# Four units of a linear-attention kernel: keys turned by TensorE instead of loaded as blocks

## The chip, the core and the metric

The kernel runs on one core of a Trainium2 chip. The metric is the device time of one execution in microseconds (us). The time before is 661.25 us, the median of three runs (660.89 to 662.71). The profile is of one further execution.

Names in the rows: PE is TensorE's matmul and PEld its weight load, DVE is VectorE, ACT is ScalarE, POOL is GpSimd, SP is SyncE, which only issues transfers (DMAs).

## The reference

Attention with a complex decay that differs per step and per key dimension, then a two-layer network on its output. B, H, S, D = 4, 8, 768, 48; the network has 3072 rows, width 384 and 2048 hidden units.

```python
mag = sqrt(a_re**2 + a_im**2); scale = minimum(mag, 0.999) / (mag + 1e-6)
ar, ai = a_re * scale, a_im * scale
for t in range(S):                      # per batch and head; S_re, S_im are D x D
    S_re, S_im = (ar[t] * S_re - ai[t] * S_im + outer(k[t], v[t]),
                  ar[t] * S_im + ai[t] * S_re)      # row d of the state turns by a[t, d]
    y[t] = q[t] @ S_re
x = y as rows (b, t) of width H * D
out = gelu(x @ w_in) @ w_out            # gelu with erf
```

All is float32, the weights come as float64.

## The kernel before, in words

**Scan.** Time is cut into eight chunks (two of 64 steps in group 0, two of 64 in group 1, two of 128 in each of the groups 2 and 3). Within a chunk the product of the decays is taken step by step by VectorE (`scan`, tiles `tt` and `bt`), for all 32 lanes of batch and head at once, in 24 slices of 8 steps. Each slice multiplies queries and keys by the product or its inverse (`towards`, `against`, tile `xt`), which makes the decay vanish from the attention inside a chunk, and writes them to a table in device memory (`kq0` to `kq3`, one per group, a row of 2 x 96 numbers per lane and step).

**Units.** The attention proper is done in 24 units: unit u is batch u % 4 and the 128 steps from (u // 4) * 128. So units 8 to 11 are the first four of group 2, units 12 to 15 read the other half of the same table. Function `unit` loads values (`vn`), keys in rows (`kn`, the first half of `kqn`), and needs keys and queries also turned, with the 96 dimensions on partitions: `kT` in the two `kp` tiles and `qT` in the two `qT` tiles, four heads each. Then come the scores (`att<-qT,kp`, eight matmuls, 16 in the records), a multiplication by the causal mask on VectorE (`kp<-att,causal`, one per four heads), the output (`att<-kp,vn`, and `att<-qT,st` for the state), and the keys times values that are added to the batch's state (`att<-vn,kqn`). From unit 6 on the state is first turned by the chunk's gain; for that its halves are exchanged by two DMAs (`m<-st`). The output goes to `xT` as a high and a low part, by ScalarE and VectorE.

**Two ways to turn.** Units under `UDT` = 8 load keys and queries in rows (one DMA, `kqn<-kq`) and turn them by TensorE (`att<-ident_r,kqn`), four heads into a bank of PSUM, with a copy to the `kp` or `qT` tile by ScalarE or VectorE (nested function `turn`). Units from 8 on load both as blocks of 32 x 32 into `blk`, which lies in the memory of `raw_all` (three DMAs of 1024 packets of 128 bytes for keys and three for queries, `raw_all<-kq`), and turn each block on VectorE (`STREAM_TRANSPOSE`). Keys in rows (`kqn<-kq`, 384 KB) are loaded beside that up to unit 19, for the state. `blk` is there once: a unit's blocks can be loaded when the unit before has turned its own.

**Network.** Nine blocks j of 2, 3, 3, 3, 3, 3, 3, 2, 2 units: `ph<-xT,wi` (nine matmuls for each of 16 hidden pieces f), gelu twice on ScalarE (`gh`, `gf`), their difference on VectorE (`gl`), then `po<-wo,gh/gl`. The first matmul of a block needs the `xT` of all of its units: block 3 holds units 8 to 10, block 4 units 11 to 13. In blocks 0 and 1 the units' work and the 32 pieces of the weights are split in high and low parts beside the network's matmuls.

**Order.** Nothing is issued where the code calls it. Class `Plan` records all calls as steps with a cost (`Plan.cost`, for a DMA also `step.data` from its packets and bytes, in `Plan.add`) and with what they wait for. `natural` ranks the steps by the longest way to the end plus an offset per kind of work (table `MORE`), `forward` lets each engine take the best ranked step that is ready, with a choice of engine for copies (`BIAS` weighs the engines), and four passes back and forth keep the order that is best by the planner's own estimate. So every instruction's place on each engine follows from these tables; each engine, SP's queue too, then works strictly in that order. Almost all rows of the profile have the line 422 of `issue`.

The choice between the two ways stands here (lines 825 and 894):

```python
if u < UDT:
    P.sync.dma_start(out=kqn, in_=...)                       # rows
...
if u >= UDT:
    P.vector.transpose(out=t[0:D2], in_=blk[0:D2, c, hh * 4:hh * 4 + 4])
```

Of the kernel before, what the change touches and what calls it, by code (L numbers as in the profile page):

```python
# [20 lines left out]
B, H, S, D = 4, 8, 768, 48  # L21
D2 = 2 * D
BH = B * H
C = 128
# [4 lines left out]
GROUPS = ((0, 64), (128, 64), (256, 128), (512, 128))  # L29
NG = len(GROUPS)  # L30
NP = 2 * NG

UNITS = [[(b, t, C)] for t in range(0, S, C) for b in range(B)]
# [24 lines left out]
def dap(t, offset, dims):  # L58
    return bass.AP(t.tensor, t.offset + offset, dims)
# [9 lines left out]
FIXED = {"vector": 0.075, "scalar": 0.098, "gpsimd": 0.149, "tensor": 0.002, "sync": 0.62}  # L69
# [6 lines left out]
TABLE = 1.3  # L76
ISSUE = 0.9
FETCH = 2.2
PACKET, BYTES = 0.5e-3, 2.96e-6

ROUND, PASS = 0.462e-3, 0.4219e-3

# [10 lines left out]
PASSES = 4  # L93
N_A = 4
WL = 0.307
UDT = 8
FILL, FROM, TO, ONE = 0.6, 50.0, 82.0, 0.217

MORE = dict(lanes0=575.74, lanes1=-377.35, lanes2=-812.79, lanes3=221.09, weights0=-149.78, weights1=-103.19, units0=636.83, units1=1302.69, units2=549.34, blocks0=-201.58, blocks1=340.05, blocks2=534.64, checks=865.08)
BIAS = dict(vector=0.07, scalar=-0.61, gpsimd=7.10)  # L100


def run(x):
# [18 lines left out]
class Plan:  # L122
# [90 lines left out]
    def cost(self, call, outs, ins):  # L213
        engine, name, _, kw = call
        if engine == "sync":
            return FIXED[engine] * (1 if 32 < outs[0].shape[0] < 128 else 0.73)
        size = lambda x: int(math.prod(c for _, c in x.ap[1:]))
        n = max(size(x) for x in outs[:1] + ins)
        each = EACH[engine]
        if engine == "tensor":  # L220
            rows, cols = (kw["lhsT"] if name == "matmul" else kw["in_"]).shape[0], size(kw["lhsT"] if name == "matmul" else kw["in_"])
            if ins[0].dtype == F32R:
                return max(0.06, n * ROUND) + 0.005 * (name == "transpose")
            if name == "transpose":
                return 0.108

            if cols <= 32:
                return max(0.035, n * PASS)
            if cols <= 64:
                return max(0.056, 2 * n * PASS)  # L230
            return max(0.17 if rows > 64 else 0.195, 4 * n * PASS + 0.006)
        elif engine == "vector" and name in ("tensor_scalar", "tensor_copy") and all(x.tensor.space != PSUM for x in ins):
            each /= 2
        t = FIXED[engine] + n * each + (ACCUM[engine] if "accum_out" in kw else 0.0)
        if engine == "scalar":
            if any(x.tensor.space == PSUM for x in ins):
                t -= FROM_PSUM
            if any(size(x) == 1 for x in ins):
                t += POINTER
        elif engine == "gpsimd" and name == "scalar_tensor_tensor":  # L240
            t = FIXED[engine] + n * 1.25e-3
        return t
# [31 lines left out]
    def natural(self):  # L274

        steps = self.steps
        rest = [0.0] * len(steps)
        nextof = {}
        for i in range(len(steps) - 1, -1, -1):
            s = steps[i]  # L280
            e, (_, cost) = next(iter(s.options.items()))
            t = max((rest[j] for j in s.after), default=0.0) + cost + AFTER[e]
            if e == "sync":
                t += ISSUE + FETCH + s.data
            if s.chain is not None:
                if s.chain in nextof:
                    t = max(t, rest[nextof[s.chain]] + cost * s.weight)
                nextof[s.chain] = i
            rest[i] = t
        return [t + MORE[s.kind] for t, s in zip(rest, steps)]  # L290

    def forward(self, rank):
# [14 lines left out]
        while len(order) < len(steps):  # L307
            best = None
            for e, waiting in pool.items():
# [8 lines left out]
                if len(steps[i].options) > 1:  # L318
                    ends = {o: max(free[o], ready[i], port[other[o]] if o in steps[i].port else 0.0) + c + BIAS[o] for o, (_, c) in steps[i].options.items()}
                    if ends[e] > min(ends.values()) + 1e-9:  # L320
# [29 lines left out]
            if e == "sync":  # L350
                channel = end = max(end + FETCH, channel) + s.data
            taken[i] = e, start, cost, end - start
            order.append(i)
            for o in s.options:
# [9 lines left out]
    def backward(self, end, taken, _):  # L364

        steps = self.steps
        left = [len(s.after) for s in steps]
        ready = [end] * len(steps)
        pool = {e: [i for i, s in enumerate(steps) if not s.after and taken[i][0] == e] for e in FIXED}
        free = dict.fromkeys(FIXED, end)  # L370
        starts = [0.0] * len(steps)
        last = lambda some: max(some, key=lambda i: (taken[i][1] + taken[i][3], i))
        for _ in steps:
            best = None
            for e, waiting in pool.items():
                if not waiting:
                    continue
                t = min(free[e], max(ready[i] for i in waiting)) - NEAR
                i = last(i for i in waiting if ready[i] >= t)
                stop = min(free[e], ready[i])  # L380
                if best is None or stop > best[0]:
                    best = stop, i, e
            stop, i, e = best
            pool[e].remove(i)
            starts[i] = free[e] = stop - taken[i][2]
            for j in steps[i].before:
                o, _, cost, whole = taken[j]
                ready[j] = min(ready[j], starts[i] - (ISSUE if "sync" in steps[i].options else AFTER[o]) - (whole - cost))
                left[j] -= 1
                if not left[j]:  # L390
                    pool[o].append(j)
        return starts
# [40 lines left out]
def lanes_and_chunks(ctx, tc, flags, a_lanes, x_lanes, v_units, w_in, w_out, out):  # L433
# [5 lines left out]
    P = Plan(nc, loose=[flags])  # L439
# [44 lines left out]
    kq = [dram.tile([64, c, 2, D2], F32, name=f"kq{g}") for g, (_, c) in enumerate(GROUPS)]  # L484


    apart = [GROUPS[g][1] == C and any(u >= UDT and GROUPS[g][0] <= t < GROUPS[g][0] + 2 * C for u, some in enumerate(UNITS) for _, t, _ in some) for g in range(NG)]

    wide = w_in.dtype == U32
    own = [ps.tile([128, 512], F32, name=f"att{i}", tag=f"att{i}")[:] for i in range(3)]  # L490
# [305 lines left out]
    def unit(u):  # L796
# [3 lines left out]
        chunks, row = [], 0  # L800
        for b, t, n in UNITS[u]:
            for i in range(NP):
                g, m = divmod(i, 2)
# [15 lines left out]
        kqn = next(kqns)  # L819
        kn, qn = kqn[:, :, 0], kqn[:, :, 1]  # L820
        vn = next(vns)
        w = 2 * D2
        _, g, m, _, size, b = chunks[0]
        base, lane = ((m * BH + b * H) * size * w, size * w) if apart[g] else (b * H * 2 * size * w, 2 * size * w)
        if u < UDT:
            P.sync.dma_start(out=kqn, in_=dap(kq[g], base, [[w, C], [lane, H], [1, w]]))
        else:
            for c in range(2):
                for j in range(D2 // 32):
                    P.sync.dma_start(out=blk[j * 32:(j + 1) * 32, c].rearrange("p h (i d) -> p (h i) d", d=32),  # L830
                                     in_=dap(kq[g], base + c * D2 + j * 32, [[w, 32], [32 * w, H * C // 32], [1, 32]]))
            if chunks[-1][0] < NP - 1:
                P.sync.dma_start(out=kn, in_=dap(kq[g], base, [[w, C], [lane, H], [1, D2]]))
        P.sync.dma_start(out=vn, in_=v_units[u])

        held = []
# [54 lines left out]
        qT, kT = [], []  # L891

        def turn(src, dst, ring, halves=(0, 1)):
            if u >= UDT:
                c = 0 if src is kn else 1
                for hh in halves:
                    t = next(ring)
                    P.vector.transpose(out=t[0:D2], in_=blk[0:D2, c, hh * 4:hh * 4 + 4])
                    dst.append(t)
                return  # L900
            some = [next(ps_att) for _ in halves]
            with P.together():
                for hh, p in zip(halves, some):
                    for j in range(4):
                        P.tensor.transpose(out=p[0:D2, j * 128:(j + 1) * 128].bitcast(F32R), in_=src[:, hh * 4 + j, :].bitcast(F32R), identity=ident_r[:])
            for p in some:
                t = next(ring)
                p = p[0:D2, :].rearrange("p (j l) -> p j l", j=4)
                P.either(("scalar", "copy", (t[0:D2], p), {}), ("vector", "tensor_copy", (t[0:D2], p), {}))
                dst.append(t)  # L910
# [73 lines left out]
        j = next(j for j in range(len(BLOCKS)) if u < first_unit[j + 1])  # L984
# [16 lines left out]
    blk = raw_all.rearrange("p i n -> p (i n)").bitcast(F32)[:, 0:16 * C].rearrange("p (c h l) -> p c h l", c=2, h=H)  # L1001
# [63 lines left out]
    for u in range(BLOCKS[0]):  # L1065
        with P.work("units0", f"u{u}"):
            unit(u)
# [250 lines left out]
```

## Time and profile before

| | |
|---|---|
| three runs, us | 661.25 (660.89 to 662.71) |
| profiled execution, us | 664.25 |
| its span, us | 662.2 |
| PE busy | 612.3 us, 92% |
| DVE busy | 482.5 us, 73% |
| ACT busy | 425.7 us, 64% |
| DMA queue 1 | 230720 packets, 100.69 MB, 65.5% of 16 engines' span |
| chain that ended last | PE 59%, DVE 18%, DMA 10%, ACT 8% |

The profiled execution lasts 2.05 us longer than its span. Shares over the whole span mix three stages: in the first VectorE's scan, the weights and the first units run, in the second the rest of the scan with the units from 8 on, in the third the network with the later units. A busy PE is one with a matmul in its records, and its ends are modelled; what an engine waits for is told apart from that in the list of waits.

### The profile page before, as it was taken

What the parts mean: (1) busy time and instruction counts of PE and PEld (TensorE: products, weight loads), DVE (VectorE), ACT (ScalarE), POOL (GpSimd) and SP (SyncE); (2) the same over time, 40 slices, a digit from 0 to 9 for tenths busy, and PEclk for the clock granted to TensorE, in tenths of its full rate; (3) what the DMA queues carried; (4) which work ended last, traced back from release to release, by engine and by line L of the source; (5) the groups of instructions that cost most, each with busy time, mean ns of one, the idle gap of its engine ahead of it and who ended that gap; (6) DMA issues with size and microseconds to landing.
All of it is one profiled execution on the core that took longest, in us unless ns stands there. A gap on an engine that the chain in (4) does not pass through costs nothing.

```text
span 662.2 us, 16181 instructions
## 1 busy us (share of the span) xinstructions
PE 612.3 (92%) x6384; PEld 560.2 (85%) x6384; DVE 482.5 (73%) x1179; ACT 425.7 (64%) x989; POOL 19.9 (3%) x65
## 2 busy tenths in 40 slices
PE   5368799999999999999799999999999999999996
PEld 2136578898899999998788999998899999999995
DVE  7999999998999999998798999436454332342211
ACT  7556678788888888855487887535554544454632
POOL 2001000003000000100100000000000000000000
PEclk9878899999999999999999999999999999999998
DMA  9178967784565556798999796899774570642000
GB/s 295 53 211 216 308 198 199 208 243 131 158 166 127 137 143 163 152 175 152 205 188 211 155 167 172 170 183 148 164 120 113 117 178 4 133 155 73 24 1 28
DMA packets 230801, 101.77 MB, mean 154 GB/s; under 512 B 182080, under 2 KB 223040, under 8 KB 230720
## 3 DMA queue, kind: packets, MB, share of 16 engines
q1 hardware_dynamic: 230720, 100.69, 65.5%
q8 instruction: 51, 0.84, 0.5%
q14 instruction: 30, 0.25, 0.1%
HBM read 74.12 MB, written 23.59 MB: 148 GB/s over the span
## 4 chain that ended last, share of the span: by engine, by line
PE 59%; DVE 18%; DMA 10%; ACT 8%; issue 3%; SPq 2%; DVEq 0%; ACTq 0%
PE po L422 24%; PE ph L422 22%; PE att L422 12%; DVE a L422 4%; DMA m<-st 3%; DVE tt L422 3%; DVE bt L422 2%; DVE xt L422 2%; SPq L422 2%; ACT a L422 2%; DVE tab L422 1%; DMA a<-in_a_lanes_dram 1%; DVE gl L422 1%; DMA kq<-xt 1%; DMA a<-in_moe_w_out_dram 1%
## 5 line engine op out<-in xcount | busy, mean ns | idle before, releaser
L422 PE MATMUL ph<-xT,wi_hi 128*128 128x384 f32 (+1 forms) x864 | 207.7, 321 | 1.9 <-ACT gh L422 1.0
L422 DVE TENSOR_TENSOR gl<-gf,gh 128x384 fp32r<-128x384 f32 (+1 forms) x144 | 73.8, 512 | 121.9 <-ACT gf L422 113.3
L422 PEld LDWEIGHTS ph<-xT,wi_hi 128*128 128x128 f32 x864 | 153.7, 188 | 5.8 <-ACT gh L422 2.0
L422 PE MATMUL ph<-xT,wi_lo 128*128 128x384 f32 (+1 forms) x432 | 137.1, 317 | 0.0
L422 PE MATMUL po<-wo_hi,gh 128*128 128x384 f32 x384 | 132.6, 345 | 3.1 <-ACT ot L422 1.9
L422 ACT ACTIVATE gh<-ph 128x384 fp32r<-128x384 f32 (+1 forms) x144 | 65.3, 455 | 107.8 <-PE ph L422 107.2
L422 PE MATMUL po<-wo_lo,gh 128*128 128x384 f32 x384 | 128.8, 335 | 0.0
L422 PE MATMUL po<-wo_hi,gl 128*128 128x384 f32 x384 | 91.1, 338 | 0.0
L422 PEld LDWEIGHTS ph<-xT,wi_lo 128*128 128x128 f32 x432 | 81.2, 188 | 0.0
L422 PEld LDWEIGHTS po<-wo_hi,gh 128*128 128x128 f32 x384 | 72.2, 188 | 7.3 <-ACT gh L422 3.2
L422 PEld LDWEIGHTS po<-wo_lo,gh 128*128 128x128 f32 x384 | 72.3, 188 | 0.1
L422 ACT ACTIVATE gf<-ph 128x384 f32<-128x384 f32 (+1 forms) x144 | 65.1, 452 | 10.6 <-DVE gl L422 9.1
L422 DVE TENSOR_TENSOR tt<-bt,a 128x192 f32<-128x192 f32 x192 | 68.1, 355 | 0.1
L422 PEld LDWEIGHTS po<-wo_hi,gl 128*128 128x128 f32 x384 | 66.0, 188 | 0.8 <-issue 0.2
L422 ACT ACTIVATE a<-a 128x384 f32<-128x384 f32 (+1 forms) x77 | 41.4, 539 | 20.1 <-DVE a L422 7.9
L422 DVE TENSOR_TENSOR bt<-tt 128x96 f32<-128x96 f32 x192 | 48.8, 254 | 0.1
L422 PEld LDWEIGHTS att<-qT,kp 96*64 96x64 f32 (+1 forms) x512 | 38.8, 164 | 7.4 <-DVE kp L422 4.3
L422 PE MATMUL att<-qT,kp 96*64 96x64 f32 (+1 forms) x512 | 41.4, 251 | 3.9 <-DVE kp L422 3.3
L422 PE MATMUL po<-raw_all,ident_r 128*128 128x384 f32 x64 | 30.4, 557 | 10.2 <-DVE raw_all L422 6.8
L422 DVE TENSOR_TENSOR kp<-att,causal 128x512 f32<-128x512 f32 x48 | 31.9, 686 | 8.2 <-PE att L422 8.0
L422 ACT ACTIVATE a<-a,by_partition 128x384 f32<-128x384 f32 x53 | 33.7, 635 | 1.2
L422 ACT ACTIVATE a<-tab 128x384 f32<-128x384 f32 (+1 forms) x45 | 23.9, 534 | 8.3 <-DVE tab L422 8.2
(157 smaller groups left out, 918.2 us busy)
## 6 DMA issues: line engine op xcount, KB each, us to landing
raw_all<-kq SPq DMA_DIRECT2D x96, 128.0 KB, 4.4
xt<-in_x_lanes_dram SPq DMA_DIRECT2D x24, 384.0 KB, 4.2
kq<-xt SPq DMA_DIRECT2D x48, 192.0 KB, 3.4
a<-in_a_lanes_dram SPq DMA_DIRECT2D x20, 384.0 KB, 4.0
raw_all<-in_moe_w_in_dram SPq DMA_DIRECT2D x16, 384.0 KB, 3.7
raw_all<-in_moe_w_out_dram SPq DMA_DIRECT2D x16, 384.0 KB, 3.8
vn<-in_v_units_dram SPq DMA_DIRECT2D x24, 256.0 KB, 3.7
kqn<-kq SPq DMA_DIRECT2D x8, 768.0 KB, 6.7
```

What stands on the lines that cost most here:

```text
L422: getattr(getattr(self.nc, engine), name)(*args, **kw)
```

## The change

Units 8 to 11 (`QDT` = 8, `KDT` = 12) load only their queries as blocks. Their keys are read in rows, which were loaded before too, and turned by TensorE as in units 0 to 7. From unit 12 on both are blocks as before. The planner's tables change with it: the cost of a packet, the cost of a DMA on SP's queue by kind, the offsets `MORE` and the weights `BIAS`.

```diff
-PACKET, BYTES = 0.5e-3, 2.96e-6
+PACKET, BYTES = 0.6e-3, 2.96e-6
-UDT = 8
+QDT, KDT = 8, 12
-MORE = dict(lanes0=575.74, ...)
+MORE = dict(lanes0=435.30, ...)
-BIAS = dict(vector=0.07, scalar=-0.61, gpsimd=7.10)
+BIAS = dict(vector=0.19, scalar=-0.10, gpsimd=5.92)
@@ def cost
-            return FIXED[engine] * (1 if 32 < outs[0].shape[0] < 128 else 0.73)
+            return FIXED[engine] * (1.06 if outs[0].shape[0] < 128 and outs[0].tensor.name[:3] != 'raw' else 0.73)
@@ def unit
-        if u < UDT:
+        if u < min(QDT, KDT):
             P.sync.dma_start(out=kqn, in_=dap(kq[g], base, [[w, C], [lane, H], [1, w]]))
         else:
-            for c in range(2):
-                for j in range(D2 // 32):
-                    P.sync.dma_start(out=blk[j * 32:(j + 1) * 32, c].rearrange("p h (i d) -> p (h i) d", d=32),
-                                     in_=dap(kq[g], base + c * D2 + j * 32, [[w, 32], [32 * w, H * C // 32], [1, 32]]))
-            if chunks[-1][0] < NP - 1:
-                P.sync.dma_start(out=kn, in_=dap(kq[g], base, [[w, C], [lane, H], [1, D2]]))
+            for c, first in ((0, KDT), (1, QDT)):
+                if u >= first:
+                    for j in range(D2 // 32):
+                        P.sync.dma_start(out=blk[j * 32:(j + 1) * 32, c].rearrange("p h (i d) -> p (h i) d", d=32),
+                                         in_=dap(kq[g], base + c * D2 + j * 32, [[w, 32], [32 * w, H * C // 32], [1, 32]]))
+                if u < first or c == 0 and chunks[-1][0] < NP - 1:
+                    P.sync.dma_start(out=kqn[:, :, c], in_=dap(kq[g], base + c * D2, [[w, C], [lane, H], [1, D2]]))
@@ def turn
-            if u >= UDT:
-                c = 0 if src is kn else 1
+            c = 0 if src is kn else 1
+            if u >= (KDT, QDT)[c]:
```

In the whole program 96 block transfers become 84, 64 VectorE transposes become 56, 128 turns on TensorE become 160, and with them eight more copies out of PSUM; 35 filler matmuls (line 415, issued in planned gaps of PE) become 29. Three places show how the order moves.

SP's queue where units 8 to 10 are fetched, before (`raw_all<-kq2` are blocks, `kqn` keys in rows, `m20<-st` the exchange of a state's halves, `kq3<-xt` a slice's rows of group 3; first row: unit 8's blocks):

```order
L422 DMA raw_all_120<-kq2_107 32x32x32 x6
L422 DMA kqn0_139<-kq2_107 128x8x96
L422 DMA m20_143<-st1_151 48x8x48 x2
L422 DMA kqn1_140<-kq2_107 128x8x96
L422 DMA xt1_133<-in_x_lanes_dram 128x8x96
L422 DMA raw_all_120<-kq2_107 32x32x32 x6
L422 DMA a30_122<-in_a_lanes_dram 128x2x384
L422 DMA m20_143<-st2_152 48x8x48 x2
L422 DMA kqn0_139<-kq2_107 128x8x96
L422 DMA vn0_141<-in_v_units_dram 128x512
L422 DMA raw_all_120<-kq2_107 32x32x32 x6
```

The same place now; unit 8's keys in rows stand just ahead of the first row, and the row of six holds three blocks of unit 12's keys and three of unit 9's queries:

```order
L422 DMA raw_all_120<-kq2_107 32x32x32 x3
L422 DMA kqn1_140<-kq2_107 128x8x96
L422 DMA m20_143<-st0_150 48x8x48 x2
L422 DMA xt1_133<-in_x_lanes_dram 128x8x96
L422 DMA raw_all_120<-kq2_107 32x32x32 x6
L422 DMA a30_122<-in_a_lanes_dram 128x2x384
L422 DMA m20_143<-st1_151 48x8x48 x2
L422 DMA kqn0_139<-kq2_107 128x8x96
L422 DMA vn0_141<-in_v_units_dram 128x512
L422 DMA kq3_108<-xt0_132 32x8x192
L422 DMA kq3_108<-xt0_132 32x8x96 x3
L422 DMA raw_all_120<-kq2_107 32x32x32 x3
```

Each unit's own blocks are half as many, keys in rows stand ahead of them, and a slice's writes have moved in front of unit 10's.

PE ahead of unit 9's scores (the last two rows), before:

```order
L422 MATMUL po0_114<-wo_hi_103,gl1_161 128x384
L422 MATMUL po1_115<-wo_hi_103,gl1_161 128x384
L422 MATMUL po2_116<-wo_hi_103,gl1_161 128x384
L422 MATMUL ph1_113<-xT0_148,wi_hi_101 128x384 x2
L422 MATMUL ph1_113<-xT0_148,wi_lo_102 128x384
L422 MATMUL po0_114<-wo_hi_103,gh0_158 128x384
L422 MATMUL po0_114<-wo_lo_104,gh0_158 128x384
L422 MATMUL ph1_113<-xT0_148,wi_hi_101 128x384 x2
L422 MATMUL ph1_113<-xT0_148,wi_lo_102 128x384
L422 MATMUL att1_110<-qT0_144,kp0_146 128x128 x4
L422 MATMUL att2_111<-qT1_145,kp1_147 128x128 x4
```

And now, from the turns of unit 9's keys (first two rows) on; its scores stand two rows below the last one shown:

```order
L422 MATMUL att0_109<-ident_r_81,kqn1_140 96x128 x4
L422 MATMUL att1_110<-ident_r_81,kqn1_140 96x128 x4
L422 MATMUL po1_115<-wo_hi_103,gh1_159 128x384
L422 MATMUL po1_115<-wo_lo_104,gh1_159 128x384
L422 MATMUL ph1_113<-xT0_148,wi_hi_101 128x384 x2
L422 MATMUL ph1_113<-xT0_148,wi_lo_102 128x384
L422 MATMUL po2_116<-wo_hi_103,gh1_159 128x384
L422 MATMUL po2_116<-wo_lo_104,gh1_159 128x384
L422 MATMUL ph1_113<-xT0_148,wi_hi_101 128x384 x2
L422 MATMUL ph1_113<-xT0_148,wi_lo_102 128x384
L422 MATMUL po0_114<-wo_hi_103,gl1_161 128x384
L422 MATMUL po1_115<-wo_hi_103,gl1_161 128x384
```

The turns are new, with 13 matmuls of the network between them and the scores.

VectorE where unit 8's keys and queries are turned, before:

```order
L422 STREAM_TRANSPOSE qT0_144<-raw_all_120 96x512
L422 STREAM_TRANSPOSE qT1_145<-raw_all_120 96x512
L422 TENSOR_TENSOR bt1_127<-tt1_131 128x2x48
L422 SCALAR_TENSOR_TENSOR tab0_128<-a32_124,tab0_128 128x384
L422 STREAM_TRANSPOSE kp0_146<-raw_all_120 96x512
L422 STREAM_TRANSPOSE kp1_147<-raw_all_120 96x512
L422 TENSOR_TENSOR tt0_130<-bt1_127,a31_123 128x192
L422 TENSOR_TENSOR a30_122<-a30_122 128x384
L422 TENSOR_TENSOR bt1_127<-tt0_130 128x2x48
```

And now:

```order
L422 COPY kp0_146<-att0_109 96x512
L422 COPY kp1_147<-att1_110 96x512
L422 TENSOR_TENSOR bt1_127<-tt1_131 128x2x48
L422 TENSOR_TENSOR a30_122<-a30_122 128x384
L422 STREAM_TRANSPOSE qT0_144<-raw_all_120 96x512
L422 STREAM_TRANSPOSE qT1_145<-raw_all_120 96x512
L422 TENSOR_TENSOR tt0_130<-bt1_127,a31_123 128x192
L422 SCALAR_TENSOR_TENSOR a30_122<-a30_122 128x384
L422 TENSOR_TENSOR gl0_160<-gf0_162,gh0_158 128x384
```

Two transposes out of `raw_all` have become two copies out of PSUM, ahead of the queries' transposes; unit 8's second product with the mask is VectorE's row 738 of the order, where it was row 732.

## Rows read from the trace of the kernel before

**Rows 1.** Busy time in three stretches: us, engines' busy (instructions), PEclk, DMA share, GB/s.

```profile
core 0: us, PE busy (x) PEld busy (x) DVE busy (x) ACT busy (x) POOL busy (x), PEclk, DMA share, GB/s
8.00:284.00 276.00, 249.86 (x2791) 209.94 (x2790) 268.80 (x711) 215.17 (x437) 11.39 (x28) 0.96 0.68 181
284.00:365.00 81.00, 73.90 (x921) 68.34 (x920) 72.96 (x171) 50.24 (x121) 1.73 (x5) 1.00 0.99 187
365.00:655.00 290.00, 286.78 (x2672) 280.89 (x2671) 136.84 (x290) 154.40 (x421) 2.80 (x10) 1.00 0.57 118
```

**Rows 2.** Waits of PE from 280 to 365: us in total, times, longest.

```profile
PE att L422 <- DVE kp L422: 4.2, 6, 2.8
PE ph L422 <- DVE xT L422: 0.6, 1, 0.6
PE att L422 <- DVE qT L422: 0.6, 1, 0.6
PE ph L422 <- ACT gh L422: 0.6, 2, 0.3
PE po L422 <- ACT ot L422: 0.5, 1, 0.5
PE ph L422 <- ACT xT L422: 0.3, 1, 0.3
PE po L422 <- ACT gh L422: 0.2, 1, 0.2
```

**Rows 3.** Timeline of PE: start us, us, what; the wait before unit 11's scores.

```profile
321.61 0.33 PE L422 MATMUL ph<-xT,wi_lo 128*128 128x384 f32 x1
321.79 0.51 PE L422 MATMUL ph<-xT,wi_hi 128*128 128x384 f32 x2
322.13 0.34 PE L422 MATMUL ph<-xT,wi_lo 128*128 128x384 f32 x1
325.28 1.94 PE L422 MATMUL att<-qT,kp 96*128 96x128 f32 x15 [2.81 <-DVE kp L422]
```

**Rows 4.** Timeline of DVE there.

```profile
318.13 0.54 DVE L422 TENSOR_TENSOR xT<-att,xT 128x384 fp32r<-128x384 f32 x1
321.56 1.30 DVE L422 STREAM_TRANSPOSE qT<-raw_all 96x512 f32<-96x512 f32 x2 [2.88 <-DMA raw_all<-kq]
...
324.52 1.29 DVE L422 STREAM_TRANSPOSE kp<-raw_all 96x512 f32<-96x512 f32 x2
```

**Rows 5.** Timeline of SP's queue, the issues for units 8 to 11.

```profile
276.87 4.74 SPq L422 DMA_DIRECT2D raw_all<-kq  x6
281.65 0.86 SPq L422 DMA_DIRECT2D kqn<-kq  x1
...
286.27 7.08 SPq L422 DMA_DIRECT2D raw_all<-kq  x6
...
298.32 7.31 SPq L422 DMA_DIRECT2D raw_all<-kq  x6
...
314.23 6.81 SPq L422 DMA_DIRECT2D raw_all<-kq  x6
```

**Rows 6.** DMA from 280 to 320: queue, packets, MB, share; issues, KB each, us to landing.

```profile
q1 hardware_dynamic: 30090, 6.67, 100.4%
raw_all<-kq SPq DMA_DIRECT2D x19, 128.0 KB, 4.6
kqn<-kq SPq DMA_DIRECT2D x4, 384.0 KB, 5.6
```

**Rows 7.** Groups of one shape: count, busy us, mean ns of one, idle before.

```profile
L422 PE MATMUL att<-ident_r,kqn 128*96 128x128 f32 x128 | 12.0, 234 | 0.4 <-DMA kqn<-kq 0.2
L422 DVE STREAM_TRANSPOSE kp<-raw_all 96x512 f32<-96x512 f32 x32 | 21.5, 694 | 5.3 <-PE att L422 3.5 <-DMA raw_all<-kq 1.5
L422 ACT COPY kp<-att 96x512 f32<-96x512 f32 x16 | 9.0, 584 | 0.9 <-PE att L422 0.4 <-PE po L422 0.3
L422 DVE TENSOR_TENSOR kp<-att,causal 128x512 f32<-128x512 f32 x48 | 31.9, 686 | 8.2 <-PE att L422 8.0 <-ACT wo_hi L422 0.2
```

**Rows 8.** Waits of PE from 365 to 640.

```profile
PE att L422 <- DVE st L422: 1.8, 1, 1.8
PE po L422 <- ACT ot L422: 1.3, 1, 1.3
```

More of the change, by code (lines that the diff above doesn't have):

```diff
@@ L95 @@
 WL = 0.307
-UDT = 8
+QDT, KDT = 8, 12
 FILL, FROM, TO, ONE = 0.6, 50.0, 82.0, 0.217
-MORE = dict(lanes0=575.74, lanes1=-377.35, lanes2=-812.79, lanes3=221.09, weights0=-149.78, weights1=-103.19, units0=636.83, units1=1302.69, units2=549.34, blocks0=-201.58, blocks1=340.05, blocks2=534.64, checks=865.08)
-BIAS = dict(vector=0.07, scalar=-0.61, gpsimd=7.10)
+MORE = dict(lanes0=435.30, lanes1=-370.28, lanes2=-936.27, lanes3=-479.30, weights0=117.89, weights1=28.10, units0=759.67, units1=993.55, units2=658.08, blocks0=-5.01, blocks1=543.97, blocks2=644.37, checks=1304.51)
+BIAS = dict(vector=0.19, scalar=-0.10, gpsimd=5.92)
 def run(x):
@@ L484, in lanes_and_chunks @@
     kq = [dram.tile([64, c, 2, D2], F32, name=f"kq{g}") for g, (_, c) in enumerate(GROUPS)]
-    apart = [GROUPS[g][1] == C and any(u >= UDT and GROUPS[g][0] <= t < GROUPS[g][0] + 2 * C for u, some in enumerate(UNITS) for _, t, _ in some) for g in range(NG)]
+    apart = [GROUPS[g][1] == C and any(u >= min(QDT, KDT) and GROUPS[g][0] <= t < GROUPS[g][0] + 2 * C for u, some in enumerate(UNITS) for _, t, _ in some) for g in range(NG)]
     wide = w_in.dtype == U32
```

## The prediction

> **What bounds the kernel now.** I read the busy time by stretches first, because the shares over the whole span mix three stages [rows 1]. From 8 to 284 us VectorE works 268.8 of 276.0 us: the scan sets the pace, 7.2 us of it are idle. From 284 to 365 us no engine is full (TensorE 73.9 of 81.0, VectorE 73.0), but the DMA share is 0.99. From 365 us on TensorE works 286.8 of 290.0 us and the DMA share is 0.57. The granted clock is 0.96, 1.00 and 1.00, so the upper of the two levels is there nearly throughout.
>
> So the change, which lies around unit 8 to 11, falls into the middle stage, and the list of TensorE's waits says what is lost there: 7.0 us in 13 waits [rows 2]. The largest group is scores that wait for VectorE (`kp`, 4.2 us in six). The longest of them, 2.81 us before unit 11's scores [rows 3], I followed to VectorE: the two transposes of the queries had themselves waited 2.88 us for `raw_all<-kq`, the blocks, and the keys' transposes came after them [rows 4]. The blocks come late for two reasons that the rows show. SP's queue is held 4.74 to 7.31 us by each six block issues [rows 5]. And the queue of transfers is full at 100.4% in 280 to 320 us, with 19 block transfers that land 4.6 us after their issue and four of keys in rows that take 5.6 us [rows 6]. The stage's bound is thus the fetching of blocks, and it costs TensorE, which has more work ready for later, some 7 us.
>
> **Removed.** Twelve block transfers go (three for each of four units); the keys in rows that replace them were loaded before. One block transfer is worth between 4.74 / 6 = 0.79 us (SP's issue pitch at its fastest [rows 5]) and 1.37 us: 1.004 x 16 x 40 us over 30,090 packets is 21.4 ns for a packet on one engine, times 1024 packets, over 16 engines [rows 6]. I take 1.0 us, near the pitch of 6.81 to 7.31 us for six. That is 12 us (9.5 to 16.4) of transfers less in a stretch that loses 7 us to them. Three blocks of unit 12 come earlier, in the same place; they take back 3 us at most, which leaves 9, still more than the waits.
>
> What does this give on TensorE? Of the 13 waits [rows 2] those of the units' chain are `kp` 4.2, `qT` 0.6, `xT` 0.6 and 0.3: 5.7 us in nine. A wait counts from the modelled end of the matmul before, but the rows show matmuls that start 0.17 to 0.18 us apart and last 0.33 or 0.34 [rows 3], so each wait hides another 0.17 us of lost pace: 9 x 0.17 = 1.5. I take 7.2 us as gone. The four waits for `gh` and `ot` (1.3 us) are the network's own and stay. Next late are the keys in rows, the queries' blocks and the mask on VectorE; the first two I price in the rivals.
>
> **Added on TensorE.** Four units have eight turns more, 32 in all. The 128 turns of before are busy 12.0 us together, 94 ns each, while one lasts 234 ns, so they overlap [rows 7]. At the pitch they cost 32 x 0.094 = 3.0 us, at their duration 32 x 0.234 = 7.5 us. I take 3.0, since the 128 are groups of four as these are. All of it is on the path, in a stage where TensorE has just got its time back. Six filler matmuls fewer I count at nothing: they stand in planned gaps of the first stage, where VectorE is the bound.
>
> **Copies.** Eight banks must be copied from PSUM: 584 ns on ScalarE, and on VectorE some 686 ns, by the mask's product, the nearest row that reads PSUM there [rows 7]. They replace eight transposes at 694 ns on VectorE [rows 7]; the three that stay on VectorE cost the same, five go to ScalarE, which is busy 50.2 of 81.0 us [rows 1]. The wait for a copy is new: between a unit's turns and its scores the order shows 13 matmuls, which at 0.17 us are 2.2 us, against 0.6 to 0.7 us for a copy. Cover gone, it would be 0.7 us for each unit, 2.8 us in all.
>
> At this point the rows give a unit's half (four heads) 694 ns by VectorE against 4 x 94 + 584 or 686, about 1.0 us, by TensorE and a copy: 0.3 us longer, eight times, 2.4 us [rows 7]. The Trainium skill, page "VectorE: DVE Perf Modes", section "Rules for kernel authors", speaks against the change too: inside 32 x 32 blocks VectorE's transpose is the fastest, and TensorE's (section "The three transpose paths") ends in PSUM. By that rule alone the sum would lose these 2.4 us. By the trace the way to the scores does not start at the transpose but at the landing that it waited 2.88 us for [rows 4], so I leave them out.
>
> **Moved on VectorE.** Six more of its instructions stand ahead of unit 8's second mask product. In the first stage an instruction takes 268.8 / 711 = 0.378 us [rows 1], so unit 8 comes up to 6 x 0.378 = 2.3 us later, or no later if the 7.2 us of idle time take them in. I take half, 1.2. More writes of slices into the tables stand in front of unit 10's blocks; they are the same transfers as before, moved. Copies of `ot` have gone to VectorE (seven instead of two), product for `gl` to other places; in a middle stage with 8 us of VectorE idle [rows 1] and 5 transposes fewer I count them at nothing; without that cover, five at 0.69 us are 3.4 us.
>
> **Last stage.** The order of the end is as before, and the two long waits there, 1.8 for `st` and 1.3 for `ot` [rows 8], stay.
>
> **Sum.** -7.2 + 3.0 + 1.2 = -3.0 us. The profiled execution took 664.25 us (span 662.2), 3.0 us above the median, so I carry the difference over: 661.25 - 3.0 = 658.25, rounded 658.3. About 0.3%, 2.0 us, is what a measurement of this kernel can tell from no change; the borders are 659.25 and 663.25.
>
> **Rivals.**
>
> First, the time is hidden anyway (near 661.3). If the scan, which keeps the transfers of group 3's slices and the masks waiting, decides when unit 11 can be done, the 5.7 us are moved to another cause and the turns fill waiting time. For it: VectorE is busy 90% even in the middle stage [rows 1]. Against: its longest wait there names the blocks [rows 4]. Then 7.2 stay, 3.0 lie inside them: no change.
>
> Second, slower: TensorE works strictly in order, and a unit's turns now stand in it before network work that is ready. If the keys in rows land later than the turn's place, TensorE stops. They land 5.6 us after issue [rows 6], and unit 8's are issued right behind the slice's writes. With 1.7 us at each of four units, 6.8 in all (under a third of a landing time, and less than the 2.81 that the blocks cost at unit 11 [rows 3]): -7.2 + 6.8 + 3.0 + 1.2 = +3.8, 665.1. It decides from 3.0 us in all, 0.75 per unit, on. Against: keys in rows are one transfer, not six, and their wait was 0.2 us before for 128 turns [rows 7].
>
> Third, the redrawn order also tightens the first stage. If half of VectorE's 7.2 us of idle time goes [rows 1] and unit 8 isn't delayed: -7.2 + 3.0 - 3.6 = -7.8, 653.5. For it: all offsets are new, and the stage has its slack on the bounding engine. Against: nothing in the steps there is removed, and 97% busy leaves little.
>
> Fourth, the turns don't overlap here and cost 7.5 us [rows 7]: -7.2 + 7.5 + 1.2 = +1.5, 662.8. Against: all turns of before overlapped. [...] The trace has 94 ns of pace, and a granted clock of 0.96 in the stage that holds all the turns [rows 1], so I give it little.
>
> That the change doesn't do what it says is excluded by the order: 84 block transfers instead of 96, 160 turns instead of 128.
>
> **How the numbers follow.** Forecast 0.46: its own range is 655.5 to 660.5 (waits that go between 5.7 and 8.7, VectorE's delay between 0 and 2.3, one copy or two uncovered), faster 0.38, no change 0.08. Hidden anyway 0.20: faster 0.02, same 0.15, slower 0.03. Keys late 0.13: same 0.01, slower 0.12. First stage tighter 0.16: faster. Turns at full duration 0.05: same 0.03, slower 0.02. Together faster 0.56, within 0.3% 0.27, slower 0.17. The range 653.0 to 664.0 takes in both unknown costs and all cases but the far part of the second and of the third rival, about 0.2.
>
> **What would show it.** Right: TensorE's waits between 280 and 365 us fall from 7.0 to about 2; VectorE has no long wait for `raw_all<-kq` there; the 160 turns are busy 15.0 us in all; unit 11's scores start near 321 to 323 us instead of 325.3. Wrong: TensorE waits for `kqn<-kq` by over 0.75 us per unit; the turns' pace is nearer 0.23 than 0.09 us; unit 8's masks come more than 2.3 us later; or the waits go and block 3 still starts as late, with VectorE's scan behind it. The third stage should keep its two waits; if the time changes there by over 1 us, the sum is right or wrong for a reason that it doesn't hold.

## The result and the profile after

The changed kernel took 652.58 us (median of four runs, 651.61 to 656.43) against 661.12 before: a ratio of 0.9877, 95% interval 0.9834 to 0.9919. Measured again beside other kernels, it was 0.9872 (0.9845 to 0.9899). So it is some 8.3 us faster, where 3.0 were forecast, and lies 0.4 us below the range of 653.0 to 664.0. Two executions of blocks_back, an experiment further down, took 698.53 and 1000.37 us in a slower state and are left out of its median and its ratio. Its profiled execution took 652.33 us, with a span of 650.2.

The same three stretches of the changed kernel, the answer to [rows 1] (this execution ends earlier, so the third row holds some empty time):

```profile
8.00:284.00 276.00, 250.96 (x2788) 209.36 (x2787) 271.04 (x718) 215.45 (x437) 10.80 (x28) 0.96 0.68 183
284.00:365.00 81.00, 81.00 (x995) 79.10 (x994) 79.70 (x189) 56.74 (x125) 3.71 (x5) 1.00 0.90 179
365.00:655.00 290.00, 277.79 (x2624) 272.59 (x2622) 129.71 (x270) 143.83 (x399) 2.45 (x10) 0.99 0.54 115
```

In the middle stage TensorE is now busy for all of the 81.0 us, where it was 73.9, and the DMA share is 0.90 instead of 0.99. The list of TensorE's waits from 280 to 365 us [rows 2] is empty, and so is that from 365 to 640 us [rows 8]: the 1.8 us for `st` and the 1.3 for `ot`, which the forecast let stay, are gone too.

The place of [rows 3 and 4], unit 11, TensorE first and then VectorE: turns, network, scores without a wait, and the queries' transposes without one.

```profile
317.85 0.69 PE L422 MATMUL att<-ident_r,kqn 128*96 128x128 f32 x8
...
320.05 2.05 PE L422 MATMUL att<-qT,kp 96*128 96x128 f32 x16
```

```profile
315.42 1.29 DVE L422 STREAM_TRANSPOSE qT<-raw_all 96x512 f32<-96x512 f32 x2
...
319.31 0.68 DVE L422 COPY kp<-att 96x512 f32<-96x512 f32 x1
```

The scores start at 320.05 us, before at 325.28. Of these 5.2 us, 2.5 are the network's earlier start in this execution (100.5 us instead of 103.0, see the table below); counted from that start the scores come 2.8 us earlier, and in the second profiles of the two kernels 1.5 us. The transfers from 280 to 320 us, against [rows 6]: the queue has fallen from 100.4% to 86.4%, and a block lands in 3.8 us instead of 4.6.

```profile
q1 hardware_dynamic: 26295, 7.08, 86.4%
...
raw_all<-kq SPq DMA_DIRECT2D x15, 128.0 KB, 3.8
kqn<-kq SPq DMA_DIRECT2D x3, 384.0 KB, 4.0
```

And the turns, against the first of [rows 7]: 32 more, 2.6 us busy more, 81 ns each.

```profile
L422 PE MATMUL att<-ident_r,kqn 128*96 128x128 f32 x160 | 14.6, 233 | 0.1
```

To see all of TensorE's time I split it, in two profiles of each kernel, from the network's first matmul to the last of all. Each matmul counts from its start to the next one's start, less the idle time between; the kinds add up to the total (us):

| | before | before, second | after | after, second |
|---|---|---|---|---|
| network starts at | 103.0 | 102.9 | 100.5 | 103.2 |
| from there to the end | 553.4 | 550.8 | 543.1 | 542.6 |
| idle | 12.8 | 9.4 | 3.7 | 3.7 |
| network | 417.6 | 417.3 | 414.3 | 414.1 |
| units without turns | 99.9 | 101.2 | 98.9 | 98.5 |
| turns | 5.4 | 5.3 | 7.4 | 7.5 |
| pieces of weights | 17.7 | 17.7 | 18.8 | 18.8 |

The mean falls by 9.2 us: idle -7.4, network and units -5.1, turns +2.1, pieces of weights +1.1 (a piece that was split before the first block is now split in it). The number of network and unit matmuls is the same.

### The profile page after: what moved, and what is told of

Same layout as the page of the kernel before. It is cut to its first block, busy times and chain, and to the rows that moved or that the text cites. A ratio compares the mean times of both kernels' runs of the same rounds, so it can differ in the third digit from the quotient of the medians.

```text
span 650.2 us, 16173 instructions
## 1 busy us (share of the span) xinstructions
PE 611.1 (94%) x6404; PEld 561.9 (86%) x6404; DVE 484.6 (75%) x1184; ACT 421.1 (65%) x970; POOL 21.0 (3%) x65
## 4 chain that ended last, share of the span: by engine, by line
PE 72%; DVE 19%; DMA 3%; issue 3%; ACT 2%; SPq 0%; DVEq 0%; ACTq 0%
PE po L422 29%; PE ph L422 27%; PE att L422 16%; DVE a L422 5%; DVE tt L422 3%; DVE bt L422 2%; DVE xt L422 2%; DVE tab L422 2%; DMA kq<-xt 1%; DVE wh L422 1%; DVE raw_all L422 1%; DVE gl L422 1%; DMA raw_all<-in_moe_w_out_dram 1%; DMA a<-in_a_lanes_dram 1%; DVE m L422 0%
```

## The experiments

"Waits" are the sums of TensorE's list in 280 to 365 and in 365 to 640 us; "net" is the time from the network's first matmul to the end, which leaves out the first stage. Ratios are to the kernel before on the same chip.

| kernel | median us | ratio (95%) | waits | starts at, net |
|---|---|---|---|---|
| before_again | 661.85 | one run | 4.6, 2.4 | 102.9, 550.8 |
| tables_only | 667.08 | 1.0081 (1.0061 to 1.0101) | 8.9, 0 | 109.2, 555.0 |
| turns_only | 654.19 | 0.9905 (0.989 to 0.992) | 1.4, 1.0 | 102.5, 544.9 |
| turns_only_again | 654.44 | 0.9876 (0.9854 to 0.9898) | 0, 1.2 | 106.6, 544.2 |
| after_again | 654.14 | 0.9872 (0.9845 to 0.9899) | 0.2, 0 | 103.2, 542.6 |
| rows_both | 664.48 | 1.0063 (1.0047 to 1.0078) | 1.7, 0 | 109.2, 545.2 |
| no_key_blocks_9 | 654.9 | 0.9898 (0.9876 to 0.9919) | 1.1, 2.1 | 104.9, 545.3 |
| few_packets | 657.6 | 0.9953 (0.9938 to 0.9968) | 2.3, 2.6 | 102.9, 546.5 |
| no_key_blocks_12 | 659.14 | 0.9972 (0.9954 to 0.999) | 3.9, 3.0 | 102.9, 548.9 |
| no_key_blocks_16 | 658.46 | 0.995 (0.9936 to 0.9965) | 4.1, 0.2 | 102.7, 546.4 |
| no_key_blocks_both | 651.72 | 0.9854 (0.9839 to 0.987) | 0.7, 0 | 102.7, 540.5 |
| blocks_back | 660.55 | 0.9998 (0.9975 to 1.0021) | 4.4, 0.8 | 106.4, 551.4 |
| turns_twice | 657.27 | 0.9934 (0.9907 to 0.9962) | 0, 0 | 100.5, 545.2 |
| k10 | 664.5 | 1.0037 (1.0018 to 1.0056) | 3.1, 0.9 | 104.6, 550.0 |
| k16 | 665.31 | 1.0053 (1.0037 to 1.0068) | 2.3, 0 | 106.2, 549.7 |

**Which part of the change.** Theory: fewer block transfers end the waits. Rival: the redrawn order does.

before_again, without an edit: 

> The kernel before once more, for a second profile. Theory A (all waits belong to the order): the waits of TensorE return as in the first profile, 7.0 us in 280 to 365 us and 1.8 for st and 1.3 for ot after 365. Theory B (part of the 664.25 us of the first profiled execution was an accident): the two waits after 365 us are gone or under 1 us, and the run is near 661.

Its waits, in 280 to 365 us and then in 365 to 640 us:

```profile
PE att L422 <- DVE kp L422: 4.0, 5, 2.8
PE ph L422 <- DVE xT L422: 0.6, 1, 0.6
...
PE po L422 <- ACT ot L422: 1.4, 1, 1.4
PE att L422 <- DVE st L422: 1.0, 1, 1.0
```

These waits return, so they belong to the kernel, though the sum in the middle is 4.6 us and not the expected 7.0. The wait before unit 11's scores is 2.8 us again.

tables_only, new tables without the turned keys:

```diff
-QDT, KDT = 8, 12
+QDT, KDT = 8, 8
```

> New tables and costs of the planner, but units 8 to 11 load keys and queries as blocks, as before. Theory A (the fetch of blocks is what was removed): the waits between 280 and 365 us stay at 5 to 8 us, time 657 to 661. Theory B (the order made the gain, the turned keys little): 652 to 655, waits there under 3 us.

It was 5.4 us slower than before, with 8.9 us of waits in the middle. The waits stay, as theory A has it, but the time lies outside both expectations; in its profile the network starts 6 us later (109.2 us), so part of the loss is in the first stage. turns_only has the other half, the turned keys under the old `PACKET`, `cost`, `MORE` and `BIAS`:

> Keys of units 8 to 11 turned by TensorE, with the old tables and costs of the planner. Theory A (the fetch of blocks): waits between 280 and 365 us fall under 2 us, block 0 starts at 103 as before, 655 to 658. Theory B (the order): near 661, waits there stay over 4 us.

```profile
PE po L422 <- DVE gl L422: 1.4, 1, 1.4
```

That is all of its waits from 280 to 365 us; none is for `kp`. The rival falls: the tables alone lose, the keys alone win 6.3 us (0.0095 of 661). What the tables add was measured side by side:

> The changed kernel once more, beside turns_only_again, for what the tables are worth on top of the turned keys, and for a second profile. If the tables gain in the first stage: 1 to 2.5 us less than turns_only_again, first block starting at 100 to 101 us against 102 to 103. If not: within 1 us of it.

> Turned keys with the old tables, once more. 654 to 655, no wait of TensorE for kp between 280 and 365 us, and none for st after it.

0.9872 and 0.9876: nothing that can be told apart. The network's earlier start in the first profile of the changed kernel (100.5 us) didn't return either: 103.2 in its second, and 102.5 and 106.6 in the two of turns_only. That stretch scatters from run to run, and "net" is what is to be compared.

**The transfers or what goes with them.** In the kernels without key blocks the steps are planned as ever and some are then left out when they are issued, so that the order of all others stays:

```diff
+            if getattr(s, "skip", False):
+                continue
...
+                    P.steps[-1].skip = c == 0 and 9 <= u < 12
```

> The kernel before, its order unchanged, but the nine transfers of key blocks of units 9 to 11 are not issued (VectorE turns what unit 8's left there, so the scores of these units are not the reference's). Nothing else is added or moved. Theory A (the fetch of blocks makes the waits): TensorE's waits in 280 to 365 us fall from 5 to 7 us to under 2, and time by 5 to 7 us, to 654 to 656. Theory B (scan or order sets the pace, blocks are hidden anyway): over 659.

```profile
PE po L424 <- ACT gh L424: 0.8, 2, 0.6
PE att L424 <- DVE kp L424: 0.3, 2, 0.2
```

```profile
PE att L424 <- DVE st L424: 1.1, 1, 1.1
PE po L424 <- ACT ot L424: 1.0, 1, 1.0
```

Nine transfers fewer and nothing else: 6.7 us. The middle waits go (first list, 280 to 365 us), the later ones stay (second, 365 to 640 us). The counter-test puts nine such fetches into the changed kernel, with TensorE's and VectorE's order and the turns as they are:

```diff
+                    if 9 <= u < 12:
+                        P.steps[-1].ahead = [... dma_start(out=dap(kq[0], ...), in_=dap(kq[g], base + j * 32, [[w, 32], [32 * w, H * C // 32], [1, 32]])) ...]
```

> The changed kernel, its order unchanged, but ahead of the keys in rows of units 9 to 11 the three key blocks each are fetched again, nine transfers of 1024 packets of 128 bytes, into memory of the chip's DRAM that nothing reads. Theory A (the transfers themselves cost the time, not the VectorE transposes or the order): TensorE's waits between 280 and 365 us come back by 2 us or more, time 3 to 6 us over the changed kernel's 652.6 to 654.1. Theory B (the order or the engine that turns makes the gain): within 1 us of it.

```profile
PE att L422 <- DVE kp L422: 3.9, 3, 3.2
PE ph L422 <- ACT xT L422: 0.3, 1, 0.3
PE po L422 <- ACT gh L422: 0.2, 1, 0.2
```

```profile
q1 hardware_dynamic: 31802, 6.98, 100.7%
...
kq<-kq SPq DMA_DIRECT2D x9, 128.0 KB, 4.3
```

The gain is gone (0.9998), TensorE waits for `kp` by 3.9 us again, and the queue is full (280 to 320 us, 100.7%). VectorE waits 3.9 us in all for `raw_all<-kq`, as it did 4.2 us before. It overshoots the expected 3 to 6 us: the nine cost 8 us. These copies also write to DRAM; whether that is the reason was not tried. So the transfers are the cause, by removing and by adding; a block cost 6.7 / 9 = 0.75 us in the one direction and 0.9 in the other.

Whether it is their packets or their number:

```diff
+                    if c == 0 and 9 <= u < 12:
+                        P.steps[-1].instead = [... out=blk[...][:, 0:4], in_=dap(..., [[w, 32], [32 * w, 4], [1, 32]]) ...]
```

> As no_key_blocks_9, but the nine transfers are issued with 128 packets instead of 1024 (one eighth of the block; the scores of units 9 to 11 are not the reference's). If the packets' time is what costs (in the queue of transfers or in SP's issue, which would then shorten with them): like no_key_blocks_9 within 1 us. If SP's time for each issue costs, whatever the transfer's size: at least half of the waits stay, 657 to 660.

```profile
285.65 6.10 SPq L422 DMA_DIRECT2D raw_all<-kq  x6
296.44 5.21 SPq L422 DMA_DIRECT2D raw_all<-kq  x6
309.44 6.25 SPq L422 DMA_DIRECT2D raw_all<-kq  x6
```

```profile
289.15 4.55 SPq L424 DMA_DIRECT2D raw_all<-kq  x3
298.74 2.79 SPq L424 DMA_DIRECT2D raw_all<-kq  x3
310.37 3.35 SPq L424 DMA_DIRECT2D raw_all<-kq  x3
```

A gain of 3.1 us, nearly half of the 6.7: both count. SP's queue (first list: few_packets, second: no_key_blocks_9, units 9 to 11) is held 5.2 to 6.3 us by six issues although three of them carry an eighth, and 2.8 to 4.6 us by three. Read issue by issue, most of the first list is the three query blocks, which stand first in each row (3.5 to 4.4 us). The three small ones take 1.4 to 2.1 us, where the full key blocks of the kernel before took 2.4 to 3.2 us: an eighth of the packets leaves some 60% of SP's time.

**The last stage's waits.** no_key_blocks_12 leaves out the key blocks of units 12 to 15 in the same way, no_key_blocks_16 those of units 16 to 19, and no_key_blocks_both those of 9 to 11 and 16 to 19.

> The kernel before, its order unchanged, without the twelve transfers of key blocks of units 12 to 15 (their scores are not the reference's). Theory A (blocks make the waits of the last stage too): the waits for st and ot after 365 us (2.4 to 3.1 us) go, those from 280 to 365 us stay, time 657.5 to 659. Theory B (the two waits belong to the order and not to the transfers): 660 to 661.5.

> The kernel before, its order unchanged, without the twelve transfers of key blocks of units 16 to 19 (their scores are not the reference's). Units 16 and 17's blocks stand right ahead of the exchange m<-st for whose end TensorE waits near 448 us. Theory A (the blocks hold SP's queue there): the wait for st goes, 1.0 to 2.2 us, and time is 658.5 to 660. Theory B (the exchange stands too near its use in the order): wait and time stay, 660.5 to 662.

> The kernel before, its order unchanged, without the key blocks of units 9 to 11 and of 16 to 19 (their scores are not the reference's). If the middle stage's and the last stage's waits are separate and both come from blocks: the sum of the two, 6.7 + 1 to 2.5, so 652 to 653.5. If the last stage's waits stay: 654 to 655.

```profile
PE att L424 <- DVE kp L424: 2.8, 4, 1.9
PE ph L424 <- DVE xT L424: 0.6, 1, 0.6
PE ph L424 <- ACT xT L424: 0.5, 1, 0.5
...
PE att L424 <- DVE st L424: 2.2, 1, 2.2
PE po L424 <- ACT ot L424: 0.8, 1, 0.8
```

This is no_key_blocks_12: the expectation missed, since the waits for `st` and `ot` stay, and most of those before 365 us too; the time, 1.9 us under before, lies between its two ranges. SP's queue ahead of the exchange, in the second profile of before, in no_key_blocks_16 and in the changed kernel:

```profile
431.33 6.96 SPq L422 DMA_DIRECT2D raw_all<-kq  x6
438.39 0.76 SPq L422 DMA_DIRECT2D a<-in_moe_w_out_dram  x1
439.25 1.30 SPq L422 DMA_DIRECT2D m<-st  x2
```

```profile
427.98 3.19 SPq L424 DMA_DIRECT2D raw_all<-kq  x3
431.22 0.60 SPq L424 DMA_DIRECT2D a<-in_moe_w_out_dram  x1
434.66 1.30 SPq L424 DMA_DIRECT2D m<-st  x2
```

```profile
424.59 6.67 SPq L422 DMA_DIRECT2D raw_all<-kq  x6
431.31 0.91 SPq L422 DMA_DIRECT2D a<-in_moe_w_out_dram  x1
432.31 1.30 SPq L422 DMA_DIRECT2D m<-st  x2
```

The matmuls that use the state, in the same three kernels:

```profile
445.92 1.08 PE L422 MATMUL att<-qT,st 96*32 96x128 f32 x32 [1.02 <-DVE st L422]
```

```profile
442.98 1.06 PE L424 MATMUL att<-qT,st 96*32 96x128 f32 x32
```

```profile
439.35 1.06 PE L422 MATMUL att<-qT,st 96*32 96x128 f32 x32
```

Blocks of units 16 and 17 hold SP's queue for 7 us ahead of `m<-st`. With half of them the wait is gone and the kernel 3.3 us faster; with units 9 to 11's gone too it is 9.7 us, close to the sum of 6.7 and 3.3 (both times are just below their ranges). The exchange's first transfer then lands 2.3 us after its issue instead of 4.6. In the changed kernel these blocks are still there, 6.67 us long, and that transfer still takes 4.5 us, so it is not a freer queue that helps. What differs is the distance: from the exchange's issue to its use 439.35 - 432.31 = 7.0 us (6.4 in its second profile), against 445.92 - 1.02 - 439.25 = 5.65 before, where it is wanted (5.1 in the first profile). So the new order hides there what blocks cost. In turns_only, under the old tables, this wait is gone too, but in another way: the last block is issued by 429.75 us, the exchange at 434.40, and it lands after 2.3 us. So the changed list of steps is enough under either set of tables; which step moved the exchange and its use was not tried.

**The price of the turns.** The changed kernel, the new turns issued twice:

```diff
+            P.steps[-1].times = 2 if 8 <= u < 12 else 1
```

> The changed kernel, its order unchanged, each of the 32 new turns issued twice in a row (same values to the same bank). Price of a turn: 94 ns by the forecast, so +3.0 us; 64 ns by the growth of the turns' time in the trace (5.4 to 7.4 us after the first block's start), so +2.1; 234 ns by the duration, so +7.5. All over the changed kernel's 652.6.

```profile
L422 PE MATMUL att<-ident_r,kqn 128*96 128x128 f32 x192 | 16.9, 233 | 0.1
```

Busy time grows by 16.9 - 14.6 = 2.3 us for 32, 72 ns each, and "net" by 2.1 us over the changed kernel's first profile, 2.6 over its second; both exclude 7.5. The times alone (-2.5 to -6.1 us against before, where the changed kernel is at -8.3) scatter too much to tell 2.1 from 3.0.

**More or fewer units.** rows_both is `QDT, KDT = 12, 12`, k10 `8, 10` and k16 `8, 16`, each planned with the new tables.

> As the changed kernel, but units 8 to 11 take their queries in rows too and turn them by TensorE: 12 block transfers fewer, 32 turns and 8 copies more, and 384 KB more of rows for each unit. If block fetches still bound the middle stage in the changed kernel: faster than it by 1 to 4 us. If TensorE has no wait left there, only the turns count: 32 x 0.094 = 3 us slower, 655 to 657.

> As the changed kernel, but only the keys of units 8 and 9 are turned by TensorE. If half the relief is enough: 16 turns less, 1.0 us faster than the changed kernel. If the blocks of units 10 and 11 bound again: waits for kp come back at units 10 and 11, 1 to 4 us slower.

> As the changed kernel, with the keys of units 12 to 15 turned by TensorE too. If TensorE has nothing left to win from fewer blocks: 32 turns more at 64 ns, so 2.1 us slower than the changed kernel, 653.5 to 656 (the order is drawn anew, which can add to it at the first block's start). If blocks still cost time: no slower than the changed kernel.

All three times lie outside what was expected. rows_both was 4.2 us slower than before, but not by its units: net it is 545.2, 2.1 to 2.6 over the changed kernel, with turns of 10.0 us instead of 7.4. The network starts 6 us or more later, at 109.2. In k10 3.1 us of waits come back, most of them for `kp`:

```profile
PE att L422 <- DVE kp L422: 1.9, 2, 1.7
PE ph L422 <- DVE xT L422: 1.0, 1, 1.0
```

(280 to 365 us.) They are not the waits of before. The longest, 1.7 us, stands ahead of `att<-kp,vn`, that is, TensorE waits for the mask's product; VectorE was busy with other work ahead of it and waited for blocks for 0.5 us in all, against 4.4 us before. So k10 doesn't show that the blocks of units 10 and 11 bind again. k16 has net 549.7, some 7 us over the changed kernel, 2.5 of them turns. In k10 and k16 the order was drawn anew in every stage, so the time doesn't settle which number of units is best; that is open. Of the five lists of steps that were drawn with the new tables only the changed kernel's gained; the other four (tables_only among them) were 2.4 to 5.4 us slower than before.

## Why the prediction was wrong

**What bounds the middle stage: right.** That the fetching of blocks makes TensorE's waits was shown from both sides (no_key_blocks_9, blocks_back). One block was taken at 1.0 us of transfer time; left out or put back it was worth 0.75 to 0.9 us of the kernel's.

**Removed: right in kind, too small.** The forecast took nine waits of 5.7 us plus 1.5 us of pace as gone and kept those for `gh` and `ot` in the middle. All went: 7.0 us by the list in the first profile, 4.6 in the second. The second lost 1.5 us of this difference in pace; the granted clock fell there (below).

**Last stage: the step that failed.** "The order of the end is as before, and the two long waits there, 1.8 for `st` and 1.3 for `ot`, stay." They went, 2.4 to 3.1 us by the two profiles. I had read that stage by its mean DMA share of 0.57 [rows 1], but in 420 to 440 us it is 1.10 in the profile that I read and 1.08 in the second, and the exchange stands there behind six blocks (the second):

```profile
420.00:440.00 20.00, 20.00 (x124) 19.95 (x123) 7.02 (x13) 7.62 (x21) 1.23 (x5) 1.00 1.08 184
440.00:460.00 20.00, 18.98 (x308) 18.08 (x307) 9.76 (x18) 9.28 (x28) 0.00 (x0) 1.00 0.98 152
```

The order of the end is the same only from 617.5 us of before's profile on (by the tiles' names, TensorE's last 265 matmuls); it says nothing on 440 us, where the exchange and its use had moved apart. The prediction had set its own sign for this: a change of over 1 us in the third stage means a reason that the sum doesn't hold.

**Pace: the term that missed by most.** Network and units became 5.1 us shorter, against 1.5 in the forecast. I cut the four profiles at the same network matmuls, those that start at 280 and at 365 us in the first. The network is 2.4 us shorter between the two and 0.9 after them. The units' 1.8 us can't be cut so, since a unit's work moved across the border. The loss that the forecast priced is in it, and larger: in the first profile of before 12 of the network's matmuls between the cuts stand directly ahead of an idle stretch and take 2.1 us more than the usual pitch, in the second 7 with 1.3 us, in the changed kernel none. The second profile's lower clock is in it too. What makes the rest is open.

**Turns: 3.0 forecast, 2.1 to 2.3 measured.** The forecast divided a busy time, in which the modelled end of each group counts. Counted from start to start, as in the table, the 128 turns of before take 9.4 us, 73 ns each, and 32 more in groups of eight cost 64 to 72 ns each. The fourth rival (234 ns each) is excluded.

**VectorE's delay: right in size, but it doesn't count.** Against the network's start unit 8's second mask product came 186.9 and 186.0 us later before, and 188.2 and 188.3 after: 1.3 to 2.3 us, where 1.2 was taken out of up to 2.3. But TensorE had network work to do meanwhile; no wait for it is in its list. I added a delay of an engine that wasn't waited for to the path, 1.2 us.

**Rivals.** Hidden anyway: no. Keys in rows too late: the changed kernel has no wait for them between 280 and 640 us. The tighter first stage, which would have brought 653.5, gave the nearest time for the wrong reason: the first stage gave nothing that returned.

So the sum's -3.0 misses by 0.9 (turns), 1.2 (VectorE), 1.7 (idle in the forecast -5.7, measured -7.4, the last stage the reason), 3.6 (pace) and -1.1 (a piece of weights moved in): 6.3, which gives -9.3, and the profiles have -9.2; the runs, with the first stage's scatter in them, say -8.3.

## What to carry to other kernels

A stage's mean share of the transfers hides stretches in which the queue is full; look at it in slices of 20 us or less around every wait on the bounding engine, before a wait is said to stay. A delay counts only where the bounding engine has no other work in its order at that point. Tables fitted to one list of steps are to be judged with that list alone: the same tables lost up to 5.4 us with another.

## What the runs showed of the hardware

A wait on TensorE can cost its clock as well. In the second profile of before the stretch with the 2.8 us wait is followed by one at the lower of the two levels (0.50, 1.2 GHz):

```profile
320.00:325.00 5.00, 2.15 (x12) 1.83 (x11) 4.78 (x10) 1.37 (x3) 0.00 (x0) 0.89 1.06 251
325.00:330.00 5.00, 5.00 (x21) 5.00 (x21) 5.00 (x13) 1.89 (x5) 0.00 (x0) 0.50 1.10 201
330.00:335.00 5.00, 5.00 (x124) 4.69 (x124) 3.72 (x10) 3.95 (x15) 0.00 (x0) 0.93 1.06 207
```

TensorE had been busy for 2.15 of 5 us. In the first profile it was busy for 2.47 of the same 5 us, and the clock stayed at 1.00; the changed kernel, busy throughout, has 1.00 in all three. The fall is no accident of one execution: the profiles of tables_only, blocks_back, k10, no_key_blocks_12 and no_key_blocks_16 have it too between 320 and 340 us, each in or just after a wait of 1.7 to 3.2 us, and no profile of the changed kernel or of turns_only has it there.

SP's time for one issue is not a constant. Read one by one, the six blocks that start at 298.32 us [rows 5] hold SP for 0.38, 1.38, 2.59, 0.51, 1.23 and 0.93 us. A full queue alone doesn't make an issue long: in the changed kernel a single block at 319.16 us took 0.43 us, where the DMA share was 1.16 (319 to 321 us). Fewer packets shorten it in part (few_packets, above); what else sets it is open.
